# Window attention, then two expert layers: one weight conversion a chunk in the first block, its low part on VectorE, three conversions begun in the attention's last steps

## The chip, the cores and the metric

The kernel runs on one core of a Trainium2 chip. A core has a matrix engine (PE), a vector engine (DVE), an activation engine (ACT), a general engine (POOL) and an engine that only issues transfers (SP); each works through a queue of its own, in order, and waits on semaphores for the others. The metric is device time of one launch in microseconds (us), the median of three runs.

## The reference

Three stages follow one another, all in float32. The output of the first, transposed to 2304 tokens of 512 features, goes through two expert layers with a hidden width of 2048.

```python
scores = where(0 <= i - j < 128, q @ k.T / sqrt(64) + slope * -|i - j|, -1e9)   # 4 x 8 heads, 576 x 64
x = (softmax(scores) @ v).transpose(0, 2, 1, 3).reshape(2304, 512)

h = x @ moe_w_in                                        # first layer, 512 -> 2048
P = a[0] + a[1]*h + a[2]*h*h + a[3]*h*h*h
Q = 1 + |b[0]|*|h| + |b[1]|*h*h
x = (P / (Q + 1e-6)) @ moe_w_out                        # 2048 -> 512

h = x @ moe2_w_in                                       # second layer
out = where(h > 0, h, exp(min(h, 0)) - 1) @ moe2_w_out
```

The weights reach the kernel as float64 words: each weight is two 32-bit words, and the kernel makes a float32 value of them itself.

## The kernel before

**Split products.** Every large product is done in three passes of a reduced-precision float32 type: operands are split in a high part (a rounded copy) and a low part (operand minus high part), and high x high, low x high and high x low are summed in PSUM. So each operand of PE needs both parts before its group of matmuls can run.

**The weight tiles.** The first layer has 32 weight tiles, 16 of `w_in` ("wi", f = 0 to 15) and 16 of `w_out` ("wo"). A tile is loaded raw (512 KB) and converted by a chain: a scaled copy of the high words on ACT (`conv_scale`, line 174), a shift of the low words on DVE (`conv_shift`, line 182), shift-and-or of the two on DVE (`conv_or`, line 192), rounding to the high part on ACT (`conv_hi`, line 202), and the low part, a subtraction of two 128x512 operands (`conv_lo`, line 206), on POOL. The list `order` gives the sequence: wi0, wi1, wi2, wo0, wi3, wo1, wi4, and so on. Fifteen tiles are converted inside the attention stage, by steps of its hand-written queues. The other 17 are, in this order: wo6, wi9, wo7, wi10, wo8, wi11, wo9, wi12, wo10, wi13, wo11, wi14, wo12, wi15, wo13, wo14, wo15. They are left to `conv_step`. Each call of `conv_step` advances three tiles by a stage: it emits the rounding of the oldest and the scaled copy of a new one on ACT at once, and puts the low part of the oldest and the shift and or of the middle one in a list, `put_off`, out of which later code takes one at a time (`go_on`) or all. A tile whose scaled copy is in call n has its rounding and its low part in call n + 2, so 17 tiles take 19 calls.

**The first layer.** Tokens come in 5 blocks and the hidden width in 16 chunks of 128, so chunk s (0 to 79) is block s // 16, hidden rows s % 16. For each s the loop calls `gemm1(s)` (12 matmuls with tile wi, line 333), then `gemm2_T(s - 3)` (12 matmuls with tile wo, line 876), then `rational(s)`. PE runs them in this order: gemm1(s), gemm2_T(s - 3), gemm1(s + 1), and so on. The chunks 0 to 3 have their gemm1 in the attention's last steps already. `rational(s)` does, on ACT, four functions of h (lines 357 to 360) and, after DVE has the denominator (line 369), logarithm and exponential for the reciprocal (lines 372, 373); on DVE it finishes the previous chunk's quotient and its low part (lines 366, 377, 382; the last product, line 383, is on POOL from chunk 3 on) and the numerator of its own (lines 385, 386). In the first block it takes one put-off instruction at each of three places (ahead of line 366, ahead of line 377, and behind it). gemm2_T(s - 3) needs the high part of line 366 and the low part of line 383, both done in `rational(s - 2)`.

**Where the 17 conversions stand.** No call of `conv_step` at s = 0 and 1, two a chunk at s = 2 to 5, one a chunk at s = 6 to 16. At the last chunk of a block, `split_x` rounds the next block's x (ACT, line 312) and subtracts (two on DVE, two on POOL, line 313). From block 1 on, `joins` decides in which chunks weights of the second layer are prepared: none in chunks 0 and 15 of a block, none at s = 17 and s = 40. Their first three loads (`load_half`) are issued at s = 16. They use the three buffers that the conversions' scaled copies (`cvt`) used before.

**The order.** All engines' queues are written out by the program: in the attention by `QUEUES` (steps per engine, with a lag in units) and `NEEDS`, a loop that lets each step out once what it needs has been emitted; in the expert layers by the order of the calls. Steps of the attention that this text names: `r0c`, `r1a`, `XC` (ACT: parts of the first two rational functions, and a copy of attention output), `XY` (DVE: the copy of the last rows). A unit is one pair of heads, u = 0 to 15. `loads` issues the raw tiles: one a unit when a unit's q and k are done with (`load_some(1)`), four when u = 14 is done with v, the rest at u = 15.

Of the kernel before, what the change touches and what calls it, by code (L numbers as in the profile page):

```python
# [47 lines left out]
    "C10": (5,),  # L48
    "C11": (0, 3, 10, 11, 12, 14, 15),
}  # L50

ALL_S = ("S0", "S1", "S2", "S3", "S4")
NEEDS = {
# [34 lines left out]
def kernel(  # L88
# [14 lines left out]
    B, H, S, D = q.shape  # L103
# [8 lines left out]
    KF = DFF // P  # L112
# [30 lines left out]
    to_load, to_conv = order[:], order[:]  # L143
# [6 lines left out]
    def load_w(key):  # L150
        w, f = key
        w_in, w_out = ((w1_in, w1_out), (w2_in, w2_out))[f // KF]
        f %= KF
        RAW[key] = raw = place(key, [P, 2 * PC], I32, "raw")
        if w == "wi":
            nc.sync.dma_start(
                out=raw.rearrange("p (k c) -> p k c", k=KD),
                in_=w_in[:, f * P:(f + 1) * P].bitcast(I32).rearrange("(k p) c -> p k c", p=P),
            )
        else:  # L160
            nc.sync.dma_start(out=raw, in_=w_out[f * P:(f + 1) * P, :].bitcast(I32))
# [6 lines left out]
    def words(key):  # L168
        raw = RAW[key].rearrange("p (c t) -> p c t", t=2)
        return raw[:, :, 0], raw[:, :, 1]  # L170
# [5 lines left out]
    def conv_scale(key):  # L176
        T32[key] = t = cv_tile([P, PC], F32, "cvt")
        high = words(key)[1].bitcast(F32)
        scale_words(t, high)
# [6 lines left out]
    def conv_shift(key):  # L186
        shift(words(key)[0])

    def conv_or(key):
        low, _ = words(key)  # L190
        ti = T32[key].bitcast(I32)
        nc.vector.scalar_tensor_tensor(  # L192
            out=ti, in0=ti, scalar=3, in1=low, op0=ALU.logical_shift_left, op1=ALU.bitwise_or
        )

    def conv_hi(key, eng="A"):
        del RAW[key]
        WT[key] = w = place(key, [P, 2, PC], F32R, "w")
        if eng == "D":
            nc.vector.tensor_copy(w[:, 0], T32[key])  # L200
        else:
            nc.scalar.activation(out=w[:, 0], in_=T32[key], func=AF.Copy)

    def conv_lo(key, eng="G"):
        w, t = WT[key], T32.pop(key)
        (nc.vector if eng == "D" else nc.gpsimd).tensor_tensor(
            out=w[:, 1], in0=t, in1=w[:, 0].bitcast(F32), op=ALU.subtract
        )
# [4 lines left out]
    put_off = []  # L213

    def go_on():
        if put_off:
            put_off.pop(0)()

    def conv_step(keys, more=True, later=False, eng="A"):
        while put_off:  # L220
            go_on()
        if not (keys or stage["scaled"] or stage["whole"]):
            return
        new = keys.pop(0) if keys and more else None
        scaled, whole = stage["scaled"], stage["whole"]
        stage["scaled"], stage["whole"] = new, scaled
        if whole:
            conv_hi(whole, eng)
        if new:
            conv_scale(new)  # L230
        if whole:
            put_off.append(lambda: conv_lo(whole))
        if scaled:
            put_off.append(lambda: conv_shift(scaled))
            put_off.append(lambda: conv_or(scaled))
        while put_off and not later:
            go_on()

# [15 lines left out]
    WB = 512  # L254
# [27 lines left out]
    def width(c):  # L282
        return BL[c // KF][1]
# [39 lines left out]
    NCH = NB * KF  # L323
# [3 lines left out]
    def gemm1(c, f, x, b):  # L327

        conv_until(to_conv, ("wi", f))
        h_t[c] = h = bank(b, [P, width(c)], "h")  # L330
        for kk in range(KD):
            for n, (wp, xp) in enumerate(PASS):
                nc.tensor.matmul(  # L333
                    h, lhsT=WT["wi", f][:, SEL[wp], kk * P:(kk + 1) * P], rhs=x[xp][kk],
                    start=(kk == 0 and n == 0), stop=(kk == KD - 1 and n == 2),
                )
            yield

    def run_all(steps):
        for _ in steps:  # L340
            pass
# [88 lines left out]
    def attention():  # L430
        with ExitStack() as es:
# [6 lines left out]
            NU = len(units)  # L438
# [291 lines left out]
            def load_some(n):  # L730
                for _ in range(n):
                    load_w(to_load.pop(0))

            def loads(step, u):
                if step in ("qT", "kT", "zT") and {(n, u) for n in ("qT", "kT", "zT")} <= gone:
                    if u + 3 < NU:
                        load(u + 3, "qk")
                    if u < NU - 1:
                        load_some(1)
                    if u == 0:  # L740
                        nc.sync.dma_start(out=a_sb, in_=moe_a.partition_broadcast(P))
                        nc.sync.dma_start(out=b_raw, in_=moe_b.partition_broadcast(P))
                elif step in ("V0", "V1", "Y") and {(n, u) for n in ("V0", "V1", "Y")} <= gone:
                    if u + 2 < NU:
                        load(u + 2, "v")
                    else:
                        load_some(4 if u < NU - 1 else len(to_load))

            x1[0] = {}
            ahead = early()  # L750
# [41 lines left out]
            def warm(n):  # L792
                t = bank(3, [P, 4 * P], "warm")
                for _ in range(n):
                    nc.tensor.matmul(t, lhsT=zero[:, 0:P], rhs=zero, start=True, stop=True)
# [38 lines left out]
            def ready(step, u):  # L834
                wait = needs.get((step, u), []) + [
                    (n[0], u + n[1]) if isinstance(n, tuple) else (n, u) for n in NEEDS.get(step, ())
                ]
                return all(x in gone or not 0 <= x[1] < NU or not runs(*x) for x in wait)

            while any(queues.values()):  # L840
                for engine, queue in queues.items():
                    if queue and ready(*queue[0]):
                        step, u = queue.pop(0)
                        gone.add((step, u))
                        if step[0] in "xgro":
                            end_step(step)
                        elif step in CONV:
                            key = order[u - 1]
                            if step == "s0":
                                to_conv.remove(key)  # L850
                            CONV[step](key)
                        else:
                            RUN[step](u)
                        loads(step, u)
                        if (step, u) == ("kT", 0):
                            warm(1)
                        if (step, u) == ("E4", 2):
                            nc.scalar.activation(out=b_abs, in_=b_raw, func=AF.Abs)
# [7 lines left out]
    def experts():  # L866
# [29 lines left out]
        LAST = NCH - KF  # L896
# [15 lines left out]
        joined, half, two, whole, pair = {}, {}, {}, {}, []  # L912
# [32 lines left out]
        def join_shift(n):  # L945
            shift(half[n].rearrange("p (c t) -> p c t", t=2)[:, :, 0])
# [454 lines left out]
        def joins(s):  # L1401

            f = s % KF
            if s >= NCH or f in (0, KF - 1) or s in (KF + 1, 2 * KF + 8) or s < KF or width(s) < WB or s >= LAST + 3:
                return 0
            return 2 if s < LAST else 1

# [7 lines left out]
        for s in range(NCH):  # L1415
            o = s - SK
            j, f = divmod(s, KF)
            for _ in range(0 if s < 2 or s > KF else 2 if s < 6 else 1):
                conv_step(to_conv, later=True)
            if s >= 4:  # L1420
                run_all(gemm1(s, f, x1[j], (4, 5, 7)[(s - 4) % 3]))
            if f == KF - 1 and j + 1 < NB:
                x1[j + 1] = split_x(j + 1, lows="DDGG")
            if o >= 0:
                gemm2_T(o)
            if joins(s) == 2:

                def begin():
                    join_scale(nj + 1)
                    join_shift(nj)  # L1430

                rational(s, beside=(
                    begin, lambda: join_end(nj), lambda: join_shift(nj + 1), lambda: join_end(nj + 1),
                ))
            elif joins(s):
                rational(s, beside=(lambda: join_shift(nj), lambda: join_end(nj)) + 2 * (lambda: None,))
            elif s >= LAST:
                prepare(s)
            else:
                rational(s, beside=(go_on, lambda: None, go_on, go_on))  # L1440
            nj += joins(s)
            if s == KF:
                for n in range(3):
                    load_half(n)
            if joins(s + 1):
                join_scale(nj)
# [8 lines left out]
    with tc.manual_schedule():  # L1455
        attention()
        experts()
# [30 lines left out]
```

## Time and profile before

| | us |
|---|---|
| median of 3 runs (lowest, highest) | 935.35 (934.89, 935.69) |
| the profiled execution, whole | 935.59 |
| its span, first to last instruction | 933.8 |
| PE busy in the span | 912.6 (98%) |
| DVE busy | 785.1 (84%) |
| ACT busy | 706.3 (76%) |
| POOL busy | 225.0 (24%) |

All times in the text are microseconds from the start of the span of the one profiled execution. The attention takes the first 146 us, the first layer runs to about 545, the second layer to the end. A row of the timeline has the start, the length, the engine, the line, the operation with its operands, and, in brackets, how long the engine sat idle before it and who ended that. On DVE and ACT the next instruction starts a little before the one ahead has ended, so the text speaks of steps: from one start to the next.

### The profile page before, as it was taken

To read this page: it belongs to the slowest core of one execution; us is meant where nothing else is said; L and a number is where in the kernel's file an instruction comes from. 1 tells how busy PE (TensorE), PEld (TensorE's weight loads), DVE (VectorE), ACT (ScalarE), POOL (GpSimd) and SP (SyncE) were. 2 spreads that over 40 slices of the span, in tenths; PEclk is the share of its full clock that TensorE was granted. 3 is DMA by queue.
4 is the path that set the end of the run, shared out by engine and by line. 5 is a ranking of instruction groups with operands and counts; after the bars stand their busy time and mean duration, and the time that the engine had idled before them with its cause. 6 is when DMAs were issued, how large, how long until landed. Compare 5 with 4: busy or idle time off the path is not lost.

```text
span 933.8 us, 15528 instructions
## 1 busy us (share of the span) xinstructions
PE 912.6 (98%) x5110; PEld 774.7 (83%) x5110; DVE 785.1 (84%) x1709; ACT 706.3 (76%) x1500; POOL 225.0 (24%) x279
## 2 busy tenths in 40 slices
PE   8999998898999999999999999999999999999998
PEld 5777776686788888889988888898989888888887
DVE  7878887899899989997899889999968688777653
ACT  6898986888788888779887877675877567766553
POOL 4677782443422322232322210000000000000000
PEclk9999999899899999999999999999999999999999
DMA  9986647000155334410010133545243323442201
GB/s 194 205 201 167 161 139 271 1 1 0 52 152 159 113 92 146 131 62 1 1 35 0 38 93 99 167 158 194 88 158 105 121 80 102 147 147 79 80 1 67
DMA packets 112176, 98.27 MB, mean 105 GB/s; under 512 B 62432, under 2 KB 85984, under 8 KB 112096
## 3 DMA queue, kind: packets, MB, share of 16 engines
q1 hardware_dynamic: 109568, 96.56, 35.5%
q10 hardware_dynamic: 2528, 0.72, 0.4%
q8 instruction: 40, 0.66, 0.3%
q14 instruction: 40, 0.33, 0.1%
HBM read 79.96 MB, written 17.30 MB: 104 GB/s over the span
## 4 chain that ended last, share of the span: by engine, by line
PE 85%; DVE 11%; issue 2%; ACT 1%; POOL 1%; DVEq 0%; POOLq 0%; ACTq 0%
PE acc L1102 21%; PE m L1086 18%; PE acc L876 17%; PE h L333 17%; PE ps_pT L652 3%; PE s_ps L578 3%; PE x L671 3%; PE ps_qk L522 2%; DVE space_g L366 2%; DVE cvt L192 1%; DVE xT L369 1%; DVE xT L386 1%; DVE h L385 1%; DVE xT L382 1%; PE s_ps L560 1%
## 5 line engine op out<-in xcount | busy, mean ns | idle before, releaser
L876 PE MATMUL acc<-space_g,w_wo 128*128 128x512 f32 (+1 forms) x960 | 216.5, 374 | 8.6 <-POOL space_g L383 8.4
L876 PEld LDWEIGHTS acc<-space_g,w_wo 128*128 128x128 f32 x960 | 170.5, 192 | 42.4 <-POOL space_g L383 11.3
L383 POOL TENSOR_TENSOR space_g<-xT,space_r 128x512 fp32r<-128x512 f32 (+1 forms) x78 | 92.0, 1180 | 267.2 <-DVE xT L382 212.1
L1102 PE MATMUL acc<-op_wo,space_g 128*128 128x512 f32 x432 | 108.3, 393 | 0.0
L333 PE MATMUL h<-space_qa,w_wi 128*128 128x512 f32 (+1 forms) x320 | 93.0, 375 | 2.6 <-ACT space_qa L312 2.6
L1102 PEld LDWEIGHTS acc<-op_wo,space_g 128*128 128x128 f32 x432 | 80.5, 188 | 14.7
L1148 ACT ACTIVATE space_u<-space_r 128x384 f32<-128x384 f32 x48 | 25.1, 522 | 75.3 <-DVE space_r L1142 74.5
L1086 PE MATMUL m<-xo_wi,op_wi 128*128 128x384 f32 x336 | 77.3, 337 | 0.0
L333 PE MATMUL h<-space_qb,w_wi 128*128 128x512 f32 (+1 forms) x240 | 76.7, 374 | 0.5 <-DVE space_qb L313 0.5
L1086 PE MATMUL m<-xo_wo,op_wi 128*128 128x384 f32 x336 | 76.4, 335 | 0.0
L333 PE MATMUL h<-space_ta,w_wi 128*128 128x512 f32 (+1 forms) x240 | 76.2, 372 | 0.0
L357 ACT ACTIVATE space_u<-h 128x512 f32<-128x512 f32 (+1 forms) x78 | 43.0, 552 | 36.4 <-PE h L333 25.6
L369 DVE SCALAR_TENSOR_TENSOR xT<-space_u,b_abs,qa 128x512 f32<-128x512 f32 (+1 forms) x76 | 52.1, 685 | 21.7 <-ACT qa L358 21.6
L366 DVE TENSOR_TENSOR space_g<-xT,space_r 128x512 fp32r<-128x512 f32 (+1 forms) x79 | 65.1, 824 | 5.7
L333 PEld LDWEIGHTS h<-space_qa,w_wi 128*128 128x128 f32 x320 | 58.4, 191 | 13.1 <-ACT space_qa L312 3.0
L1086 PEld LDWEIGHTS m<-xo_wo,op_wi 128*128 128x128 f32 x336 | 60.9, 188 | 4.1
L372 ACT ACTIVATE space_r<-xT,c_q 128x512 f32<-128x512 f32 (+1 forms) x78 | 53.8, 690 | 11.6 <-DVE xT L369 11.5
L1086 PEld LDWEIGHTS m<-xo_wi,op_wi 128*128 128x128 f32 x336 | 60.6, 188 | 0.0
L333 PE MATMUL h<-space_bi,w_wi 128*128 128x512 f32 (+1 forms) x160 | 59.6, 372 | 1.0 <-DVE space_bi L764 0.8
L1152 ACT ACTIVATE space_u<-space_u,c_m 128x384 f32<-128x384 f32 x96 | 57.5, 611 | 1.6
L359 ACT ACTIVATE xT<-h,a_sb 128x512 f32<-128x512 f32 (+1 forms) x78 | 57.6, 738 | 0.0
L360 ACT ACTIVATE h<-h,a_sb 128x512 f32<-128x512 f32 (+1 forms) x78 | 55.9, 716 | 0.0
(209 smaller groups left out, 2132.4 us busy)
## 6 DMA issues: line engine op xcount, KB each, us to landing
space_qa<-joined_wo SPq DMA_DIRECT2D x43, 256.0 KB, 2.7
raw_wo<-in_moe_w_out_dram SPq DMA_DIRECT2D x20, 512.0 KB, 5.2
raw_wi<-in_moe_w_in_dram SPq DMA_DIRECT2D x16, 512.0 KB, 4.9
half<-in_moe_w_in_dram SPq DMA_DIRECT2D x32, 256.0 KB, 2.7
two_wo<-joined_wi SPq DMA_DIRECT2D x32, 256.0 KB, 2.9
s<-sums SPq DMA_DIRECT2D x32, 256.0 KB, 2.7
half<-in_moe_w_out_dram SPq DMA_DIRECT2D x22, 256.0 KB, 2.9
v<-in_v_dram SPq DMA_DIRECT2D x32, 128.0 KB, 3.3
```

Of the source, the lines that this page charges most:

```text
L333: nc.tensor.matmul(h, lhsT=WT["wi", f][:, SEL[wp], kk * P:(kk + 1) * P], rhs=x[xp][kk], start=(kk == 0 and n == 0), stop=(kk == KD - 1 and ...
L357: nc.scalar.activation(out=h2, in_=h, func=AF.Square)
L359: nc.scalar.activation(out=ee, in_=h, func=AF.Identity, scale=a_sb[:, 1:2], bias=a_sb[:, 0:1])
L360: nc.scalar.activation(out=h, in_=h, func=AF.Identity, scale=a_sb[:, 3:4], bias=a_sb[:, 2:3])
L366: nc.vector.tensor_tensor(out=hi, in0=ee0, in1=rr0, op=ALU.mult)
L369: nc.vector.scalar_tensor_tensor(out=qq, in0=h2, scalar=b_abs[:, 1:2], in1=qa, op0=ALU.mult, op1=ALU.add)
L372: nc.scalar.activation(out=rr, in_=qq, func=AF.Ln, bias=c_q)
L383: (nc.gpsimd if c > 2 else nc.vector).tensor_tensor(out=low, in0=ee0, in1=rr0, op=ALU.mult)
L876: nc.tensor.matmul(acc_t[d], lhsT=WT["wo", f][:, SEL[wp], d * P:(d + 1) * P], rhs=gt[SEL[xp]], start=(f == 0 and n == 0), stop=(f == KF - ...
L1086: nc.tensor.matmul(out, lhsT=w[:, SEL[wp], c0:c0 + P], rhs=XO[q // NP2, nm, k][:, SEL[xp]], start=(k == 0 and n == 0), stop=(k == 1 and n ...
L1102: nc.tensor.matmul(acc_t[T, t], lhsT=gt[SEL[xp]][:, t * P:(t + 1) * P], rhs=w[:, SEL[wp]], start=(first and n == 0), stop=(last and n == 2),)
L1152: nc.scalar.activation(out=e, in_=e, func=AF.Identity, bias=c_m)
```

## The change

The low part of the 17 tiles that `conv_step` handles goes from POOL to DVE and stands behind the shift and the or in the put-off list. Three calls of `conv_step` are made in the attention, behind the steps `r0c`, `r1a` and `XC` of unit 15, and what they put off is emitted behind `XY` of unit 15. In the first layer there is one call a chunk at s = 2 to 17, in place of two a chunk at s = 2 to 5 and one at 6 to 16. Raw tiles 12 to 17 of the list are loaded a little earlier: two a unit at u = 11 to 13, two rather than four at u = 14. `load_half` begins at s = 17, the chunks 17 and 18 are without joins, and chunk 40 now has two.

```diff
+CONV_AFTER = (("r0c", 15), ("r1a", 15), ("XC", 15))
...
         if new:
             conv_scale(new)
-        if whole:
-            put_off.append(lambda: conv_lo(whole))
         if scaled:
             put_off.append(lambda: conv_shift(scaled))
             put_off.append(lambda: conv_or(scaled))
+        if whole:
+            put_off.append(lambda: conv_lo(whole, "D"))
...
-                        load_some(1)
+                        load_some(2 if 10 < u < 14 else 1)
...
-                        load_some(4 if u < NU - 1 else len(to_load))
+                        load_some(2 if u < NU - 1 else len(to_load))
...
+                        if (step, u) in CONV_AFTER:
+                            conv_step(to_conv, later=True)
+                        if (step, u) == ("XY", NU - 1):
+                            while put_off:
+                                go_on()
...
-            if s >= NCH or f in (0, KF - 1) or s in (KF + 1, 2 * KF + 8) or s < KF or width(s) < WB or s >= LAST + 3:
+            if s >= NCH or f in (0, KF - 1) or s in (KF + 1, KF + 2) or s < KF or width(s) < WB or s >= LAST + 3:
...
-            for _ in range(0 if s < 2 or s > KF else 2 if s < 6 else 1):
+            if 2 <= s <= KF + 1:
                 conv_step(to_conv, later=True)
...
-            if s == KF:
+            if s == KF + 1:
                 for n in range(3):
                     load_half(n)
```

PE's instructions stand in the same order in both programs. What moves is on DVE, ACT, POOL and SP. The added lines shift line numbers by 2 in the changed program up to the queues' loop and by 7 behind it: line 366 is 368 there, line 206 is 208.

DVE behind the attention, before: line 427 is chunk 0's last product, and the next rows are the first of chunk 2 (chunk 1's own part is done in the attention).

```order
L411 TENSOR_TENSOR h<-space_u,h 128x512
L412 TENSOR_TENSOR xT<-xT,h 128x512
L427 TENSOR_TENSOR space_g<-xT,space_r_75 128x512
L182 TENSOR_SCALAR raw_wo_2121<-raw_wo_2121 128x512
L366 TENSOR_TENSOR space_g<-xT,space_r_76 128x512
L369 SCALAR_TENSOR_TENSOR xT<-space_u,b_abs,xT 128x512
```

The same place in the changed program: `raw_wi_1692` and `cvt_2183` are tile wi9, `cvt_2139` is wo6, and `raw_wo_1811` is wo7.

```order
L413 TENSOR_TENSOR h<-space_u,h 128x512
L414 TENSOR_TENSOR xT<-xT,h 128x512
L429 TENSOR_TENSOR space_g<-xT,space_r_75 128x512
L184 TENSOR_SCALAR raw_wi_1692<-raw_wi_1692 128x512
L194 SCALAR_TENSOR_TENSOR cvt_2183<-cvt_2183,raw_wi_1692 128x512
L208 TENSOR_TENSOR w_wo_2258<-cvt_2139,w_wo_2258 128x512
L184 TENSOR_SCALAR raw_wo_1811<-raw_wo_1811 128x512
L368 TENSOR_TENSOR space_g<-xT,space_r_76 128x512
L371 SCALAR_TENSOR_TENSOR xT<-space_u,b_abs,xT 128x512
```

Shift and or of wi9 and the low part of wo6 have come in between chunk 0's last product and the shift of chunk 2. Shift and or of wo6 stand further ahead, right behind the step XY. On ACT the rounding of wi9 now stands ahead of chunk 2's functions of h.

DVE in one chunk of the middle of the block, before:

```order
L366 TENSOR_TENSOR space_g<-xT,space_r_75 128x512
L369 SCALAR_TENSOR_TENSOR xT<-space_u,b_abs,qa 128x512
L182 TENSOR_SCALAR raw_wo_2233<-raw_wo_2233 128x512
L377 SCALAR_TENSOR_TENSOR xT<-xT,space_g 128x512
L192 SCALAR_TENSOR_TENSOR cvt_2451<-cvt_2451,raw_wo_2233 128x512
L382 TENSOR_TENSOR xT<-xT 128x512
L385 TENSOR_TENSOR h<-space_u,h 128x512
L386 TENSOR_TENSOR xT<-xT,h 128x512
```

DVE in chunk 14 and at the begin of chunk 15 in the changed program: `w_wi_2810` is tile wi15, the operand of gemm1(15); the two rows of line 315 are the split of the next block's x.

```order
L184 TENSOR_SCALAR raw_wo_2251<-raw_wo_2251 128x512
L368 TENSOR_TENSOR space_g<-xT,space_r_76 128x512
L371 SCALAR_TENSOR_TENSOR xT<-space_u,b_abs,qa 128x512
L194 SCALAR_TENSOR_TENSOR cvt_2766<-cvt_2766,raw_wo_2251 128x512
L379 SCALAR_TENSOR_TENSOR xT<-xT,space_g 128x512
L208 TENSOR_TENSOR w_wi_2810<-cvt_2720,w_wi_2810 128x512
L384 TENSOR_TENSOR xT<-xT 128x512
L387 TENSOR_TENSOR h<-space_u,h 128x512
L388 TENSOR_TENSOR xT<-xT,h 128x512
L315 TENSOR_TENSOR space_qb<-xT,space_qa 128x512
L315 TENSOR_TENSOR space_ta<-xT,space_qa 128x512
L184 TENSOR_SCALAR raw_wo_2253<-raw_wo_2253 128x512
```

A chunk has nine DVE instructions rather than eight; the shift stands ahead of line 368, and the low part (line 208) between lines 379 and 384.

POOL near the end of the block before, where `w_wi_2771` is tile wi15, and line 383 is in turn the one of chunks 12, 13 and 14:

```order
L383 TENSOR_TENSOR space_g<-xT,space_r_76 128x512
L206 TENSOR_TENSOR w_wi_2771<-cvt_2681,w_wi_2771 128x512
L383 TENSOR_TENSOR space_g<-xT,space_r_75 128x512
L206 TENSOR_TENSOR w_wo_2817<-cvt_2727,w_wo_2817 128x512
L383 TENSOR_TENSOR space_g<-xT,space_r_76 128x512
```

In the changed program POOL has only the rows of line 385 (383 before) there and the two of the split; the low part of wi15 has gone from ahead of chunk 13's row to the middle of chunk 14 on DVE.

## Rows read from the trace of the kernel before

**Rows 1.** Waits of PE, 145 to 245 us: total, times, longest.
```profile
PE acc L876 <- POOL space_g L383: 8.4, 6, 3.2
PE h L333 <- ACT space_qa L312: 2.6, 1, 2.6
```

**Rows 2.** Windows: length, then PE, PEld, DVE, ACT, POOL busy, granted clock, DMA.
```profile
160.00:180.00 20.00, 14.45 (x52) 11.18 (x53) 15.82 (x23) 14.53 (x25) 10.39 (x8) 0.86 0.01 2
180.00:190.00 10.00, 10.00 (x36) 8.02 (x35) 9.80 (x16) 8.03 (x14) 3.38 (x3) 0.77 0.00 0
...
230.00:240.00 10.00, 7.45 (x18) 5.01 (x19) 9.97 (x14) 7.64 (x14) 6.09 (x4) 0.66 0.08 25
```

**Rows 3.** Timeline of PE, first block and start of the second.
```profile
152.00 2.88 PE L876 MATMUL acc<-space_g,w_wo 128*128 128x512 f32 x12
...
186.40 2.88 PE L876 MATMUL acc<-space_g,w_wo 128*128 128x512 f32 x12
...
191.84 2.88 PE L876 MATMUL acc<-space_g,w_wo 128*128 128x512 f32 x12
...
223.19 0.61 PE L333 MATMUL h<-space_qa,w_wi 128*128 128x512 f32 x2
...
244.21 2.88 PE L876 MATMUL acc<-space_g,w_wo 128*128 128x512 f32 x12
```

**Rows 4.** Timeline of DVE, one chunk (s = 9) and the start of the next.
```profile
196.50 1.80 DVE L366 TENSOR_TENSOR space_g<-xT,space_r 128x512 fp32r<-128x512 f32 x1
198.23 0.73 DVE L369 SCALAR_TENSOR_TENSOR xT<-space_u,b_abs,qa 128x512 f32<-128x512 f32 x1
198.89 0.42 DVE L182 TENSOR_SCALAR raw_wo<-raw_wo 128x512 int32<-128x512 int32 x1
199.22 0.68 DVE L377 SCALAR_TENSOR_TENSOR xT<-xT,space_g 128x512 f32<-128x512 f32 x1
199.83 0.68 DVE L192 SCALAR_TENSOR_TENSOR cvt<-cvt,raw_wo 128x512 int32<-128x512 int32 x1
200.43 0.68 DVE L382 TENSOR_TENSOR xT<-xT 128x512 f32<-128x512 f32 x1
201.03 0.68 DVE L385 TENSOR_TENSOR h<-space_u,h 128x512 f32<-128x512 f32 x1
201.75 0.69 DVE L386 TENSOR_TENSOR xT<-xT,h 128x512 f32<-128x512 f32 x1
202.57 1.80 DVE L366 TENSOR_TENSOR space_g<-xT,space_r 128x512 fp32r<-128x512 f32 x1
```

**Rows 5.** Timeline of POOL: chunk 3's end, chunk 9, tile wi15.
```profile
159.90 1.27 POOL L383 TENSOR_TENSOR space_g<-xT,space_r 128x512 fp32r<-128x512 f32 x1 [3.39 <-DVE xT L382]
...
196.47 1.29 POOL L206 TENSOR_TENSOR w_wi<-cvt,w_wi 128x512 fp32r<-128x512 f32 x1
201.28 1.30 POOL L383 TENSOR_TENSOR space_g<-xT,space_r 128x512 fp32r<-128x512 f32 x1 [3.52 <-DVE xT L382]
...
220.68 1.31 POOL L206 TENSOR_TENSOR w_wi<-cvt,w_wi 128x512 fp32r<-128x512 f32 x1
```

**Rows 6.** Timeline of DVE in block 1, without a conversion's low part on POOL.
```profile
268.38 0.68 DVE L366 TENSOR_TENSOR space_g<-xT,space_r 128x512 fp32r<-128x512 f32 x1
```

**Rows 7.** Timeline of DVE, chunk 0's last product, chunk 3, chunk 4's shift.
```profile
146.12 0.68 DVE L427 TENSOR_TENSOR space_g<-xT,space_r 128x512 fp32r<-128x512 f32 x1
...
156.78 0.75 DVE L369 SCALAR_TENSOR_TENSOR xT<-space_u,b_abs,xT 128x512 f32<-128x512 f32 x1 [1.71 <-ACT xT L358]
...
160.92 0.53 DVE L182 TENSOR_SCALAR raw_wi<-raw_wi 128x512 int32<-128x512 int32 x1
```

**Rows 8.** Timeline of ACT, a conversion's rounding at chunk 3.
```profile
154.50 0.63 ACT L202 ACTIVATE w_wi<-cvt 128x512 fp32r<-128x512 f32 x1 [2.24 <-DVE cvt L192]
```

**Rows 9.** Timeline of DVE, the split of x at chunk 15.
```profile
232.64 0.75 DVE L313 TENSOR_TENSOR space_qb<-xT,space_qa 128x512 fp32r<-128x512 f32 x1
...
236.68 0.73 DVE L369 SCALAR_TENSOR_TENSOR xT<-space_u,b_abs,qa 128x512 f32<-128x512 f32 x1
```

## The prediction

> **What bounds the kernel now.** I read PE's busy share first (98% of the span: little to win in general), then PE's waits. From 145 to 245 us, the first block of the first layer, PE waits 8.4 us in six places for POOL's line 383, and 2.6 for the rounded x of the next block [rows 1]. The windows show what these waits also cost: the granted clock is 0.86, 0.77 and 0.66 there [rows 2], so PE ran partly at 1.2 instead of 2.4 GHz. Taken as 0.14 x 20 + 0.23 x 10 + 0.34 x 10 = 8.5 us for the three waits of 2.6 to 3.2, a long wait is followed by up to some 2.8 us lost.
>
> Then the timelines. A pair of groups (gemm1 and gemm2_T, 24 matmuls) takes PE 191.84 - 186.40 = 5.44 [rows 3], 2.72 a group. A chunk on DVE takes 202.57 - 196.50 = 6.07 [rows 4]. So DVE is the slow one of the two; PE, which runs ahead of it by the three chunks of delay, in the end waits for what DVE and POOL hand over. PE's 24 matmuls from 152.00 (gemm2_T(1)) to 244.21 (gemm2_T(14)) are 13 pairs, 70.7 us of work in 92.2 [rows 3]. At most 21.5 us are to be had here. From 244.21 on I take both programs as equal.
>
> In the DVE chunk one row stands out: line 366 takes 1.80 [rows 4], and 0.68 in block 1 [rows 6]. It begins at 196.50, POOL's line 206 (the low part of a weight tile) at 196.47, for 1.29 [rows 5]; line 366 goes on only when that ends.
>
> **The change, part by part.**
>
> *Low part from POOL to DVE.* A 128x512 instruction on two SBUF operands has a step of 0.60 on DVE (199.83 to 200.43, [rows 4]); the low part adds one a chunk. Line 366 without POOL beside it has the 0.68 of [rows 6], so a step of 0.60 instead of 1.73. What is left on POOL is line 383, from 0.85 behind the start of line 382 (200.43, 201.28) for 1.3 [rows 4, 5]. It runs beside lines 385 and 386, which did not lengthen, and overlaps the shift, which now comes next. At 160.92 such a shift took 0.53 instead of 0.42, beside line 383 of 159.90 [rows 4, 5, 7]: 0.11 more. Chunk in steps: shift 0.33 + 0.11, line 366 0.60, line 369 0.66, or 0.60, line 377 0.60, low part 0.60, line 382 0.60, line 385 0.72, line 386 0.60: 5.42. Bounds: 5.31 without any overlap; 6.55 if line 366 keeps its 1.73. I take 5.42, the nearest rows.
>
> The Trainium skill (SBUF — State Buffer, Who interferes with whom) says that of a VectorE and a GpSimd instruction that need the shared port pair the one that starts later fully blocks, `tensor_scalar` in its two-port modes included. By that the shift would wait 0.2 for the end of line 383, a chunk would be 5.5 and the whole 1 us longer; the 0.11 measured at 160.92 decides.
>
> *The start.* Line 427 starts at 146.12 [rows 7]. Behind it: shift of wi9 at 146.73 (0.42, and 0.04 until the or, which waits for it), or at 147.2 to 147.9, then the low part of wo6. ACT's rounding of wi9 waits for that or, and chunk 2's functions of h are queued behind it, so it isn't hidden. From the rounding to line 369 it is 156.78 - 154.50 = 2.28 in chunk 3 before [rows 7, 8], so line 369 of chunk 2 is at 150.2. Chunk 2 (its line 383 is on DVE): 0.66 + 0.60 + 0.60 + 0.60 + 0.72 + 0.60 + 0.72 + 0.60 + 0.33 + 0.60 = 6.0, so line 369 of chunk 3 is at 156.2; before it was 156.78 [rows 7]. The single conversion wins nothing up to there, the two more in chunks 3 to 5 do later. Shift and or of wo6, some 1.1 us, fall in a gap of DVE in which it waits for PE; without that cover they would cost 1.1. The three scaled copies on ACT likewise.
>
> *Eleven chunks* follow: line 369 of chunk 14 at 156.2 + 11 x 5.42 = 215.8.
>
> *The wait that is late next.* gemm1(15) needs the low part of wi15. Before, POOL did it at 220.68, done 1.2 us ahead of gemm1(15) at 223.19 [rows 3, 5]. Now its call comes one chunk later, and it stands in the middle of chunk 14 on DVE: 215.8 + 0.66 + 0.60 + 0.60 + 0.68 = 218.4. PE would be there far earlier: it gets the low part of chunk 1 at 154.1, of chunk 2 at 160.9 (line 382 at 158.7, + 0.85 + 1.3), so gemm2_T(3) starts at 165.9, and from there DVE keeps PE's pace; gemm1(15) would stand at 165.9 + 8 x 5.44 + 2.72 = 212.1. So PE waits some 6 us, the first 0.9 already in gemm1(14) for wi14. Queued behind it is all of PE; nothing on DVE waits for it before chunk 15. The wait is the difference of PE's lead and DVE's place and costs PE's lead alone, so DVE's chain up to 218.4 sets the time.
>
> *To the end of the block.* From 218.4: 11 matmuls of gemm1(15), 2.5, then gemm2_T(12), gemm1(16), gemm2_T(13), gemm1(17), 4 x 2.72 = 10.9; gemm2_T(14) at 231.8. The split of x: from the first subtraction to line 369 it is 236.68 - 232.64 = 4.04 [rows 9], now with a shift in between, 0.33; it begins at 220.2 (lines 382, 385, 386 of chunk 14 behind the low part), so line 369 of chunk 15 is at 224.6 and the low part of wo13 at 227.1, 0.6 behind gemm2_T(13) at 226.5. And a wait of 6 us brings the half clock: I take the 2.8 from above, which hides the 0.6. gemm2_T(14) at 231.8 + 2.8 = 234.6; before 244.21 [rows 3]. That is 9.6 us less; 11.8 with the full clock (the 0.6 then counts).
>
> *Loads, joins.* The tiles that are needed earlier are also loaded one or more units (7 us) earlier; the first half loads are one chunk later, and so is their first use. Chunk 40 has the DVE work that its neighbours have beside PE. I take nothing for these, between -1 and +1.
>
> Sum: 935.59 - 9.6 = 926.0 for the profiled execution, which was 0.24 above the median, so 925.8.
>
> **The rivals.**
>
> *The clock holds, or PE's lead is not used up.* If a chunk on DVE were 5.31 or less, and the wait at gemm1(15) short, the clock would stay at 2.4 GHz and the split would not be late: 11 x 0.11 = 1.2 and 2.2 for the clock more, and 1 to 2 of the start: 921. For it: chunks in block 1 run without a gap. Against: wi15 stands a chunk later in any case.
>
> *Line 383 delays more than the shift.* If line 366 also loses some 0.2 each chunk, 5.62: 11 x 0.2 = 2.2, and two or three longer waits of PE at half clock; 929 to 930. For it: the shift's neighbour now is just line 366. Against: line 383 ends 2.15 behind the start of line 382, line 366 comes at 2.36.
>
> *The load on DVE decides: slower.* If line 366's 1.80 is not POOL's line 206 but line 366's own place behind line 386, the chunk is 6.55. Then line 369 of chunk 14 is at 228.3, wi15's low part at 230.9, gemm2_T(14) at 230.9 + 13.4 + 2.8 = 247.1, 2.9 later: 938.5. It decides from a chunk of 6.29 on (2.9 / 11 less). For it: DVE is busy for 9.80 and 9.97 of 10 us in two windows of the block [rows 2], and 17 instructions go onto it. Against: [rows 6].
>
> The Trainium skill (Perfetto Trace Analysis, Optimizing Scalar/DVE Operations) says that work of a saturated DVE may well be taken off it, even to GPSIMD, which speaks for this rival; and that between those two it might not help since they share a port, which speaks against it. Rows 5 and 6 agree with the second half.
>
> *It doesn't do what it says.* PE's part of the wait is only moved: what DVE gains up to chunk 14 comes back at wi15, wo13 and the split with a half clock through both groups, and the sum is within 0.2% (1.9 us, about what a measurement of this kernel can tell from no change): 934 to 937. Against: the six waits were DVE's pace, and that is faster by 0.65 a chunk.
>
> **How the numbers follow.** Forecast (922.5 to 928.5): 0.62. Clock or lead better: 0.12. Line 383 delays more: 0.13. Nothing gained: 0.06. Slower: 0.07. Faster by over 0.2%: 0.62 + 0.12 + 0.13 = 0.87; within: 0.06; slower: 0.07. The range leaves out the last two and the far end of the first rival: 920 to 931.5.
>
> **What would show it.** Right: line 366's row at 0.68 in the first block, DVE chunks of 5.4, line 369 of chunk 3 near 156; one long wait of PE in gemm1(15), for line 208 of DVE, of 5 to 6.5, with a granted clock of half behind it; waits for POOL's line 385 down to one or two near 154 and 160; gemm2_T(14) near 234.6. Wrong: line 366 still at 1.8, a wait for raw tiles or for ACT's rounding, or no wait at wi15.

## The result

The changed kernel takes 926.31 us (median of 4 runs, 926.18 to 926.45) and the one before, beside it, 935.52 (934.89 to 936.55): ratio 0.9900, interval 0.9883 to 0.9918. The forecast was 925.8 in 920 to 931.5, faster; it held. The profiled execution took 926.45 (span 924.7, mean granted clock 0.996) against 935.59 (933.8, 0.991): 9.14 us less.

PE's waits of the first block, 145 to 245 us, after (total, times, longest); before there were six for POOL and one for ACT [rows 1], and two of 0.5 and 0.2 for DVE:

```profile
PE h L335 <- DVE w_wi L208: 5.0, 2, 4.7
PE acc L883 <- DVE space_g L385: 1.7, 1, 1.7
PE acc L883 <- POOL space_g L385: 1.2, 1, 1.2
```

One long wait is left, and it names DVE's line 208, the low part that the change has put there. The windows after (length, PE, PEld, DVE, ACT, POOL busy, granted clock, DMA share, GB/s), to be held against [rows 2]:

```profile
160.00:180.00 20.00, 18.86 (x83) 15.56 (x84) 19.86 (x34) 17.99 (x30) 4.97 (x4) 1.00 0.01 1
180.00:190.00 10.00, 10.00 (x46) 8.29 (x45) 9.93 (x18) 8.88 (x16) 2.60 (x2) 1.00 0.00 0
...
210.00:220.00 10.00, 5.21 (x19) 3.79 (x18) 9.93 (x18) 9.29 (x16) 1.93 (x2) 0.90 0.00 1
220.00:230.00 10.00, 10.00 (x35) 7.95 (x34) 7.77 (x14) 6.37 (x12) 4.62 (x4) 0.76 0.00 0
230.00:240.00 10.00, 10.00 (x45) 8.26 (x44) 9.40 (x15) 7.82 (x13) 2.40 (x2) 1.00 0.29 81
```

Three stretches of half clock have become one, behind the one wait. In PE's timeline after (start, length, in brackets the idle time before), beside [rows 3]:

```profile
154.22 2.56 PE L883 MATMUL acc<-space_g,w_wo 128*128 128x512 f32 x10 [1.69 <-DVE space_g L385]
...
166.25 2.88 PE L883 MATMUL acc<-space_g,w_wo 128*128 128x512 f32 x12
...
218.63 0.80 PE L335 MATMUL h<-space_qa,w_wi 128*128 128x512 f32 x1 [4.69 <-DVE w_wi L208]
...
229.58 2.88 PE L883 MATMUL acc<-space_g,w_wo 128*128 128x512 f32 x12
...
235.02 2.88 PE L883 MATMUL acc<-space_g,w_wo 128*128 128x512 f32 x12
```

gemm2_T(14) starts at 235.02 instead of 244.21 [rows 3]: 9.19 us, which is the whole difference of the two executions (9.14). From there on they run alike: to the end it is 689.59 us before and 689.68 after, with PE busy for 685.2 in both.

A DVE chunk after (s = 10) with the shift of the next, beside [rows 4]:

```profile
199.21 0.68 DVE L368 TENSOR_TENSOR space_g<-xT,space_r 128x512 fp32r<-128x512 f32 x1
199.81 0.73 DVE L371 SCALAR_TENSOR_TENSOR xT<-space_u,b_abs,qa 128x512 f32<-128x512 f32 x1
200.47 0.68 DVE L194 SCALAR_TENSOR_TENSOR cvt<-cvt,raw_wi 128x512 int32<-128x512 int32 x1
201.07 0.68 DVE L379 SCALAR_TENSOR_TENSOR xT<-xT,space_g 128x512 f32<-128x512 f32 x1
201.68 0.68 DVE L208 TENSOR_TENSOR w_wo<-cvt,w_wo 128x512 fp32r<-128x512 f32 x1
202.28 0.68 DVE L384 TENSOR_TENSOR xT<-xT 128x512 f32<-128x512 f32 x1
202.88 0.68 DVE L387 TENSOR_TENSOR h<-space_u,h 128x512 f32<-128x512 f32 x1
203.59 0.69 DVE L388 TENSOR_TENSOR xT<-xT,h 128x512 f32<-128x512 f32 x1
204.20 0.51 DVE L184 TENSOR_SCALAR raw_wo<-raw_wo 128x512 int32<-128x512 int32 x1
204.62 0.68 DVE L368 TENSOR_TENSOR space_g<-xT,space_r 128x512 fp32r<-128x512 f32 x1
```

Line 368 (366 before) takes 0.68 instead of 1.80, and a chunk 204.62 - 199.21 = 5.41 instead of 6.07, though it has one instruction more.

### The profile page after: what moved, and what is told of

It reads as the page before. It is cut to its first block, busy times and chain, and to the rows that moved or that the text cites. A ratio compares the mean times of both kernels' runs of the same rounds, so it can differ in the third digit from the quotient of the medians.

```text
span 924.7 us, 15509 instructions
## 1 busy us (share of the span) xinstructions
PE 906.8 (98%) x5110; PEld 771.9 (83%) x5110; DVE 780.1 (84%) x1726; ACT 705.3 (76%) x1500; POOL 202.9 (22%) x262
## 4 chain that ended last, share of the span: by engine, by line
PE 91%; DVE 6%; POOL 1%; issue 1%; ACT 1%; POOLq 0%; DVEq 0%; ACTq 0%
PE acc L1109 21%; PE acc L883 20%; PE h L335 20%; PE m L1093 19%; PE ps_pT L654 3%; PE s_ps L580 3%; PE x L673 3%; PE ps_qk L524 2%; PE s_ps L562 1%; PE ty L684 1%; DVE pr_wo L606 0%; DVE cvt L194 0%; PE ty L538 0%; DVE xT L379 0%; POOL space_bi L315 0%
## 5 line engine op out<-in xcount | busy, mean ns | idle before, releaser
L883 PE MATMUL acc<-space_g,w_wo 128*128 128x512 f32 (+1 forms) x960 | 211.9, 369 | 3.0 <-DVE space_g L385 1.7
L883 PEld LDWEIGHTS acc<-space_g,w_wo 128*128 128x128 f32 x960 | 168.6, 189 | 34.4 <-DVE space_g L385 2.1
L385 POOL TENSOR_TENSOR space_g<-xT,space_r 128x512 fp32r<-128x512 f32 (+1 forms) x78 | 92.2, 1182 | 294.2 <-DVE xT L384 212.1
L368 DVE TENSOR_TENSOR space_g<-xT,space_r 128x512 fp32r<-128x512 f32 (+1 forms) x79 | 52.6, 666 | 4.6 <-ACT qa L360 0.5
```

The lines of the kernel that those rows point to most:

```text
L368: nc.vector.tensor_tensor(out=hi, in0=ee0, in1=rr0, op=ALU.mult)
L385: (nc.gpsimd if c > 2 else nc.vector).tensor_tensor(out=low, in0=ee0, in1=rr0, op=ALU.mult)
L883: nc.tensor.matmul(acc_t[d], lhsT=WT["wo", f][:, SEL[wp], d * P:(d + 1) * P], rhs=gt[SEL[xp]], start=(f == 0 and n == 0), stop=(f == KF - ...
```

## The experiments

My theory: DVE's pace in the block, and the moment at which its last low parts are done, set the time; the low part on DVE sets the pace, the earlier start of the conversions sets the moment; what is left is PE's wait for wi15 and the half clock behind it. Rivals: one half of the change does it alone; the loads and joins have a share. Ratios are against runs of the kernel before on the same chip (medians 935.5 to 935.7).

**The low part alone.** Kernel before, with the low part on DVE behind the or; still two conversions in chunks 2 to 5, none begun in the attention.

```diff
-        if whole:
-            put_off.append(lambda: conv_lo(whole))
         if scaled:
             put_off.append(lambda: conv_shift(scaled))
             put_off.append(lambda: conv_or(scaled))
+        if whole:
+            put_off.append(lambda: conv_lo(whole, "D"))
```

> The kernel before, with one part of the change: the low parts of the 17 tiles go to VectorE, behind the or; two conversions a chunk in chunks 2 to 5 stay. My theory (VectorE's line 366 was held up by POOL's line 206, and VectorE's pace sets the block): line 366 at 0.68 us in the whole first block, a VectorE chunk of 5.4 instead of 6.07 from chunk 6 on, so 8 x 0.65 = 5.2 us earlier at chunk 14, PE's small waits from 214 us on gone and the half clock at the change of block with them; gemm2_T(14) at 235 to 236 instead of 244.2, about 927 us in all. Rival (the gain comes from spreading the conversions, and the seventeen instructions only load VectorE): 935 to 940 us.

928.19 us, ratio 0.9920 (0.9906 to 0.9934): 7.3 us less, so the rival is out. It is 1.2 more than expected: at the change of block PE still waits 2.5 us in three places for the split, with a clock of 0.91 and 0.92 in 220:240, and the expectation had these waits as gone. DVE chunks with one conversion are 5.41 to 5.42 long, with two 8.0 to 8.3: line 369, and then the two longest waits of PE.

```profile
148.59 0.75 DVE L369 SCALAR_TENSOR_TENSOR xT<-space_u,b_abs,xT 128x512 f32<-128x512 f32 x1 [0.84 <-ACT xT L358]
...
156.88 0.75 DVE L369 SCALAR_TENSOR_TENSOR xT<-space_u,b_abs,xT 128x512 f32<-128x512 f32 x1 [0.88 <-ACT xT L358]
...
165.02 0.75 DVE L369 SCALAR_TENSOR_TENSOR xT<-space_u,b_abs,qa 128x512 f32<-128x512 f32 x1 [0.85 <-ACT qa L358]
```
```profile
161.67 2.60 PE L876 MATMUL acc<-space_g,w_wo 128*128 128x512 f32 x10 [3.62 <-POOL space_g L383]
...
169.67 4.14 PE L876 MATMUL acc<-space_g,w_wo 128*128 128x512 f32 x10 [2.22 <-POOL space_g L383]
```

PE waits 6.5 us in three places for line 383 (8.4 before); the name is POOL's, the lateness DVE's, whose chunk hands POOL its operand. gemm2_T(14) is at 237.14.

**The schedule alone.** The changed kernel with the low part back on POOL. It stays behind the or in the put-off list, as in the run above, so what that place does by itself is in both halves.

```diff
             put_off.append(lambda: conv_or(scaled))
         if whole:
-            put_off.append(lambda: conv_lo(whole, "D"))
+            put_off.append(lambda: conv_lo(whole))
```

> The changed kernel with the low parts of the 17 tiles back on POOL, so only the schedule is changed. My theory: line 368 stays at 1.8 us, a chunk at 6.05, chunk 14's line 371 at 156.3 + 11 x 6.05 = 222.9, the low part of wi15 late for gemm1(15) by some 4 us with a half clock behind; gemm2_T(14) near 238, about 929.5 us. With e1 that is more than the whole change gives, since both take the same slack of PE. Rival (the two parts add up): e1 and e2 together gain 9.2 us. Second rival (the schedule is all of it): 926.3 us.

930.40 us, ratio 0.9944 (0.9931 to 0.9957): 5.1 us less, 0.9 short of what was expected. DVE and POOL side by side at one chunk's begin, and PE at gemm1(15):

```profile
197.31 1.78 DVE L368 TENSOR_TENSOR space_g<-xT,space_r 128x512 fp32r<-128x512 f32 x1
```
```profile
197.06 1.48 POOL L208 TENSOR_TENSOR w_wi<-cvt,w_wi 128x512 fp32r<-128x512 f32 x1
```
```profile
219.84 0.50 PE L335 MATMUL h<-space_qa,w_wi 128*128 128x512 f32 x1 [2.00 <-ACT w_wi L204]
222.68 0.79 PE L335 MATMUL h<-space_qa,w_wi 128*128 128x512 f32 x1 [2.33 <-POOL w_wi L208]
```

Line 368 is as long as before and DVE's chunk 6.01 to 6.04. 7.3 and 5.1 make 12.4, the two together 9.2: they aren't additive. Either one takes time out of the same waits, and with both the first chunks are no longer what is late, but wi15.

**Loads and joins alone.** Kernel before with these four lines of the change.

```diff
-                        load_some(1)
+                        load_some(2 if 10 < u < 14 else 1)
...
-                        load_some(4 if u < NU - 1 else len(to_load))
+                        load_some(2 if u < NU - 1 else len(to_load))
...
-            if s >= NCH or f in (0, KF - 1) or s in (KF + 1, 2 * KF + 8) or s < KF or width(s) < WB or s >= LAST + 3:
+            if s >= NCH or f in (0, KF - 1) or s in (KF + 1, KF + 2) or s < KF or width(s) < WB or s >= LAST + 3:
...
-            if s == KF:
+            if s == KF + 1:
```

> The kernel before with only the edits that the prediction took at nothing: earlier loads of raw tiles 12 to 17, load_half one chunk later, chunks 17 and 18 without joins and chunk 40 with two. My theory: 935.5, within 1 us. Rival (earlier loads delay v and q, or chunk 40 gets too full): 936.5 to 939.

935.71 us, ratio 1.0002 (0.9993 to 1.0011): nothing.

**The half clock taken away.** The changed kernel with 22 more matmuls of 128x512 into gemm1(15)'s own bank ahead of it (which is started anew behind them).

```diff
+        if c == KF - 1:
+            for _ in range(22):
+                nc.tensor.matmul(h, lhsT=WT["wi", f - 1][:, 0, 0:P], rhs=x["hi"][0], start=True, stop=True)
```

> The changed kernel with 22 matmuls of 128x512 more, on operands that are there, into the bank that gemm1(15) is about to write (it starts anew, so they leave nothing behind): 22 x 0.227 = 5.0 us of work inside the wait of gemm1(15). My theory (the wait ends with the low part of wi15 and costs another 3.0 us by the half clock behind it): the granted clock stays at 2.4 GHz, the low part lands at the same 218.6, gemm2_T(14) at 232.0 to 232.8 instead of 235.0, 923.5 to 924 us. Rival (the half clock costs nothing since VectorE's chain, with the low part of wo13, is late anyway): 926 us. Slower if the extra matmuls end behind the low part: 926.5 to 927.5.

924.31 us, ratio 0.9881 (0.9867 to 0.9895): 2.0 us less than the changed kernel. The window at full clock, and gemm2_T(13), which had no wait of its own before:

```profile
220.00:230.00 10.00, 9.62 (x43) 7.65 (x42) 9.96 (x14) 7.31 (x13) 5.11 (x4) 1.00 0.01 2
```
```profile
227.48 2.79 PE L886 MATMUL acc<-space_g,w_wo 128*128 128x512 f32 x11 [0.38 <-DVE w_wo L208]
...
232.82 2.88 PE L886 MATMUL acc<-space_g,w_wo 128*128 128x512 f32 x12
```

gemm2_T(14) comes 2.20 earlier. The half clock took 3.0 us of the changed kernel (218.63 to 229.58 is 10.95, against 2.5 + 2.72 x 2 = 7.94 at full clock); without it wo13 is late, as the forecast had it, and gives part back.

**Each wi ahead of its wo.** The changed kernel with seven neighbours of `to_conv` swapped.

```diff
     to_load, to_conv = order[:], order[:]
+    for n in range(15, 28, 2):
+        to_conv[n], to_conv[n + 1] = to_conv[n + 1], to_conv[n]
```

> The changed kernel with seven pairs of tiles swapped in the order of conversion: each of wi9 to wi15 is converted before the wo tile that stood ahead of it, so that wi15's low part is made in chunk 13 instead of 14 and wo12's a chunk later. My theory (the 4.69 us wait of the second layer's half h for wi15's low part, and the half clock behind it, are what the change still leaves): the wait in gemm1(15) falls to about 0.5 us, the clock stays near 1 in 210:230, gemm2_T(12) now waits some 2.8 us for wo12 and gemm2_T(13) for wo13 until about 227.4; gemm2_T(14) begins at about 232.5 against 235.02, and the run takes 924 us (923 to 926). Rival: the wait is only handed from wi15 to wo12, with the same half clock behind it: gemm2_T(14) at about 235 and 926 us.

924.30 us, ratio 0.9883 (0.9867 to 0.9900); gemm2_T(14) at 232.79. The waits came as forecast, 2.39 for wo12 and 1.43 for wo13; the clock was 0.96 and 0.87 in 210:230, so the wait was not handed on at its full price.

**A fourth tile begun in the attention.** The changed kernel with one call more there and one less behind.

```diff
-CONV_AFTER = (("r0c", 15), ("r1a", 15), ("XC", 15))
+CONV_AFTER = (("r0a", 15), ("r0c", 15), ("r1a", 15), ("XC", 15))
...
-            if 2 <= s <= KF + 1:
+            if 2 <= s <= KF:
```

> The changed kernel with a fourth tile begun in the attention's last steps, and so fourteen chunks with a conversion instead of fifteen: every low part is made one chunk earlier. My theory (the end of the first block is set by the day on which the conversions finish): the wait for wi15's low part is gone, no half clock in 210:230, gemm2_T(14) at about 230.5 against 235.02, and the run takes about 922 us, if the fourth shift, or and low part fit into VectorE's idle time ahead of the first chunk's chain (late by 0 to 0.6 us). Rival: VectorE has no room there, its chain begins 1.6 us or more later, every chunk with it, and the gain shrinks to 0 to 2 us: 924 to 926 us.

924.40 us, ratio 0.9880 (0.9865 to 0.9894): a miss by 2.4, inside the range of the rival. Of the wait for wi15 only 0.3 us is left in gemm1(15), but DVE's chain (line 424) begins at 143.27 instead of 141.99, and PE now waits 2.5 us for the split, with a clock of 0.83 behind it.

**Both.** The fourth tile and the swapped neighbours in one kernel, by the two edits above.

> The fourth tile and the swapped pairs together. If both waits (wi15 and the wo tiles behind it) are gone with the fourth tile alone, the swap adds nothing: within 0.5 us of the kernel with the fourth tile. If the fourth tile leaves a wait for wi15, the swap takes 1 to 2 us more off; if a swapped wo tile is now the late one, it costs up to 1 us.

924.37 us, ratio 0.9881 (0.9866 to 0.9896): the swap adds nothing to the fourth tile. Four different cures stop at 924.3 to 924.4, so something else is late there. In each of the four, at the block's end, a DVE row of 0.68 takes 1.76 to 1.78 and the shift 1.49 to 1.52. DVE and POOL in the kernel with the swapped pairs:

```profile
221.10 1.76 DVE L317 TENSOR_TENSOR space_ta<-xT,space_qa 128x512 fp32r<-128x512 f32 x1
222.78 1.52 DVE L186 TENSOR_SCALAR raw_wo<-raw_wo 128x512 int32<-128x512 int32 x1
```
```profile
220.96 1.35 POOL L317 TENSOR_TENSOR space_bi<-xT,space_qb 128x512 fp32r<-128x512 f32 x1 [0.33 <-ACT space_qb L316]
222.27 1.75 POOL L317 TENSOR_TENSOR space_bi<-xT,space_ta 128x512 fp32r<-128x512 f32 x1
```

POOL's two subtractions of the split stretch a subtraction on DVE from 0.69 to 1.76 and the shift from 0.42 to 1.52: the same collision that the change has taken out of line 366. So I put them on DVE as well, for the second block's split only:

```diff
-                x1[j + 1] = split_x(j + 1, lows="DDGG")
+                x1[j + 1] = split_x(j + 1, lows="DDDD" if j == 0 else "DDGG")
```

With the swapped pairs:

> The kernel with the swapped pairs, and all four low parts of the second block's split on VectorE instead of two on GpSimd. That kernel came out at 924.3 us, as did the ones with the fill and with the fourth tile; in all three VectorE's work at the block's end runs beside GpSimd's two subtractions and is stretched: a split's subtraction 1.76 us instead of 0.69, the shift behind it 1.52 instead of 0.42. My theory (this is the new bound, since chunk 15's line 373 and the low part of wo13 stand behind it): two subtractions more cost VectorE 1.2 us and 2.1 us of stretch go; line 373 of chunk 15 starts at about 223.9 against 224.82, gemm2_T(13) gets wo13 at 226.5 instead of 227.42, gemm2_T(14) starts at about 231.9 against 232.79, and the run takes 923.4 us. Rival: VectorE's time at the block's end isn't the bound, or the subtractions cost more than the stretch: 924.3 to 925.5.

923.34 us, ratio 0.9875 (0.9858 to 0.9891); line 373 of chunk 15 at 223.85, gemm2_T(13) goes on at 226.45, gemm2_T(14) starts at 231.79, 0.05, 0.05 and 0.11 earlier than expected. With the fourth tile:

> The kernel with the fourth tile, and all four low parts of the second block's split on VectorE. There TensorE waits 2.5 us in the second block's first half h for parts of the split, and gets half a clock behind it. My theory: the parts come at 222.4, 223.0, 223.6 and 224.2 (the second was at 224.16, the last at 225.3), gemm2_T(13) starts at 226.3 to 226.6 against 227.37, gemm2_T(14) at about 232 against 232.90, and the run takes 923.4 us; a little less if the clock stays up. Rival: TensorE waits for the split until VectorE's chunk has ended anyway and the half clock stays: 924.3 to 925.

922.62 us, ratio 0.9862 (0.9847 to 0.9877). This median lies between two pairs: 921.83 and 921.91, with a mean granted clock of 1.000, and 923.33 and 923.47, with 0.998. The profiled execution is the one of 923.47 (923.4 expected), with gemm2_T(13) at 226.18, gemm2_T(14) at 232.00 and a clock of 0.83 in 220:230.

**The same with a fill ahead of the second block's first h.** 8 matmuls on a weight tile where PE waits for the split.

```diff
+        if c == KF:
+            for _ in range(8):
+                nc.tensor.matmul(h, lhsT=WT["wi", f][:, 0, 0:P], rhs=WT["wi", f][:, 0, 0:width(c)], start=True, stop=True)
```

> The kernel with the fourth tile and all four low parts on VectorE, with 8 extra 128x512 matmuls on a weight tile into the second block's first bank ahead of its h, where TensorE waits 1.8 us for the split's parts; the bank is started anew behind them, so they add nothing to a result. There gemm1(16) took 5.5 us (220.65 to 226.18) instead of 2.72, at half a clock. My theory: the clock stays at 1.00 in 220:230, gemm1(16) goes as the parts come (the last at 224.3), gemm2_T(13) starts at about 224.9 instead of 226.18, gemm2_T(14) at 230.4 to 230.8 instead of 232.00, and the run takes 921.2 to 921.6 instead of 922.6 us. Rival: VectorE's chain holds gemm2_T(13) and (14) anyway, and the time stays within 0.4 of 922.6.

921.85 us (921.76 to 921.93), ratio 0.9851 (0.9837 to 0.9864): the best version of this study, 4.5 us below the changed kernel. Clock 1.00 in 220:230, and gemm2_T(13), (14):

```profile
224.90 2.88 PE L886 MATMUL acc<-space_g,w_wo 128*128 128x512 f32 x12
...
230.34 2.88 PE L886 MATMUL acc<-space_g,w_wo 128*128 128x512 f32 x12
```

gemm2_T(14) has moved by 1.66, and the profiled execution is 923.47 - 921.85 = 1.62 shorter. The medians differ by 0.8 only, because two of the four executions without the fill took 921.8 to 921.9 already. So the fill does not beat the better executions; with it all five are like them.

**The shift back behind line 371.** The changed kernel with another order of the put-off steps.

```diff
-                rational(s, beside=(go_on, lambda: None, go_on, go_on))
+                rational(s, beside=(lambda: None, lambda: None, go_on, lambda: (go_on(), go_on())))
```

> The changed kernel with the shift of a chunk back behind line 371, so that line 368, a product of two operands in SBUF, is what follows line 388 and meets the end of GpSimd's line 385. In the changed kernel the shift there took 0.51 us instead of 0.42 and ended 0.29 behind GpSimd; line 368 beside GpSimd's low part (the kernel with it back on GpSimd) ended 0.54 behind it. Theory A (VectorE's instruction gets through its first 0.13 us and then stands until GpSimd has ended, whichever instruction it is): line 368 takes about 0.77 instead of 0.68, a VectorE chunk stays at 5.41, and the time at 926.3. Theory B (only the shift loses something): 5.32 a chunk, the low part of wi15 1.0 us earlier (216.9), 925.3. Theory C (line 368 loses the whole overlap of 0.22 or more): 5.5 a chunk or more, wi15's low part 1 to 2 us later, 927 to 928.

927.44 us, ratio 0.9910 (0.9897 to 0.9924): 1.1 us more than the changed kernel, a chunk of 5.55, wi15's low part at 219.85. These are theory C's numbers, but not its cause:

```profile
155.14 0.69 DVE L388 TENSOR_TENSOR xT<-xT,h 128x512 f32<-128x512 f32 x1
155.93 0.69 DVE L368 TENSOR_TENSOR space_g<-xT,space_r 128x512 fp32r<-128x512 f32 x1
...
199.56 0.69 DVE L388 TENSOR_TENSOR xT<-xT,h 128x512 f32<-128x512 f32 x1
200.38 0.69 DVE L368 TENSOR_TENSOR space_g<-xT,space_r 128x512 fp32r<-128x512 f32 x1
```

Line 368 is not stretched. It starts 0.82 behind line 388, whose result it reads; at 155.14, in a chunk whose line 385 is on DVE and POOL is idle, it is 0.79. An independent instruction in between has a step of 0.61 (203.59 to 204.20 above). So the shift's new place fills a gap of some 0.2 a chunk, which [rows 4] show before as well (201.75 to 202.57). That gap kept line 368 out of the collision, so line 368 doesn't tell the three theories apart. Another row of this run does, the first subtraction of the split, which also reads two operands in SBUF:

```profile
221.30 1.28 POOL L385 TENSOR_TENSOR space_g<-xT,space_r 128x512 fp32r<-128x512 f32 x1 [4.29 <-ACT cvt L176]
```
```profile
222.38 0.76 DVE L315 TENSOR_TENSOR space_qb<-xT,space_qa 128x512 fp32r<-128x512 f32 x1
```

It overlaps line 385 by 0.20 and takes 0.76 instead of 0.68, ending 0.56 behind it. That is theory A; theory B would leave it at 0.68, theory C would make it 0.88.

## Why the prediction was right, point by point

*Line 366 and the chunk.* 0.68 forecast and measured, step 0.60; chunk 5.42 against 5.41. The 0.60 that it took for line 386 rests on the shift behind it, which it did not say: with line 368 there it is 0.82.

*The shift beside POOL.* 0.11 forecast; measured 0.42 - 0.33 = 0.09, so size and sum were right. The reason was half wrong: the forecast took the 0.11 as evidence against blocking. The Trainium skill (SBUF — State Buffer, Who interferes with whom) says that of two instructions that need the shared pair the later one fully blocks. The ends of the rows agree with that: POOL's line 385 ran from 203.12 (below) to 204.42, the shift ended at 204.71, 0.29 later; [rows 5, 7] give 161.17 and 161.45, 0.28; the split above 224.02 and 224.30, 0.28, although POOL ran on for 1.24 there. Likewise line 368: 0.54 behind POOL's end in [rows 4, 5], 0.55 in the schedule alone. So of 0.42 and of 0.68 some 0.13 is as good as done before the block, and the loss is the overlap less 0.13. Where POOL's row lies after:

```profile
203.12 1.30 POOL L385 TENSOR_TENSOR space_g<-xT,space_r 128x512 fp32r<-128x512 f32 x1 [4.12 <-DVE xT L384]
```

*The start, the chain, the late wait.* Chunk 2's line 369 (371 after) at 150.2, chunk 3's at 156.2, wi15's low part done at 218.4: measured 150.28, 156.35 and 217.89 + 0.68 = 218.57.

```profile
150.28 0.75 DVE L371 SCALAR_TENSOR_TENSOR xT<-space_u,b_abs,xT 128x512 f32<-128x512 f32 x1 [0.88 <-ACT xT L360]
...
156.35 0.74 DVE L371 SCALAR_TENSOR_TENSOR xT<-space_u,b_abs,xT 128x512 f32<-128x512 f32 x1
...
217.89 0.68 DVE L208 TENSOR_TENSOR w_wi<-cvt,w_wi 128x512 fp32r<-128x512 f32 x1
...
225.00 0.75 DVE L371 SCALAR_TENSOR_TENSOR xT<-space_u,b_abs,qa 128x512 f32<-128x512 f32 x1 [1.97 <-ACT qa L360]
```

PE was to wait some 6 us in two places; it was 5.0. gemm2_T(3) came nearly on time (165.9, 166.25), but gemm1(15) began at 213.44 instead of 212.1. gemm2_T(3) gave 0.35 of that; the wait for wi14's low part in gemm1(14) put gemm2_T(11) back by 0.6 (the forecast had this wait, at 0.9, but left it out of its 212.1); and the first matmul of gemm1(15) waited 0.3 for the high part of wi15, which ACT had ready at 213.38, a wait that the forecast didn't have. It cost nothing, as PE's lead is lost in the wait anyway.

*The half clock.* 2.8 taken from the waits of before; 3.0 measured, and the fill shows that the net price was 2.0 to 2.2, as wo13 was late behind it. That the half clock hid wo13's 0.6 was right.

*The split.* Line 369 (371) of chunk 15 was forecast at 224.6 and came at 225.00, but that it came so near is luck. The 4.04 taken from [rows 9] holds two rows that POOL's subtractions stretch to 1.76; first they are shown before, then after, where POOL's subtractions come later:

```profile
233.32 1.76 DVE L313 TENSOR_TENSOR space_ta<-xT,space_qa 128x512 fp32r<-128x512 f32 x1
235.00 1.76 DVE L366 TENSOR_TENSOR space_g<-xT,space_r 128x512 fp32r<-128x512 f32 x1
```
```profile
221.40 0.69 DVE L315 TENSOR_TENSOR space_ta<-xT,space_qa 128x512 fp32r<-128x512 f32 x1 [0.22 <-ACT space_qa L314]
...
222.34 0.68 DVE L368 TENSOR_TENSOR space_g<-xT,space_r 128x512 fp32r<-128x512 f32 x1
```

The 2.15 us saved there went into a step that the forecast didn't have: DVE waited 0.22 and 1.97 us for ACT. ACT writes the next block's x over the parts that gemm1(15) still reads, and gemm1(15) was at half clock. The last three of four roundings each wait 0.65 for it:

```profile
220.74 0.63 ACT L314 ACTIVATE space_qa<-xT 128x512 fp32r<-128x512 f32 x1 [0.65 <-PE h L335]
```

*gemm2_T(14)* at 234.6: 235.02. *Loads and joins* at nothing: 0.02% alone.

*The rivals.* The slower one (DVE's own load decides) falls with the low part alone: 17 instructions more on DVE, and 7.3 us less. Its condition, that line 366's 1.80 comes from its place behind line 386, falls with two runs: in the schedule alone the shift stands between and line 368 takes 1.78, and with the shift moved back line 368 follows line 388 at once and takes 0.69. "Nothing gained" falls with the 9.2 us. Of the two that lie to either side, line 368 beside line 385 did not come true; the better clock is what the fills made, 924.31 alone and 921.85 with the fourth tile and the split on DVE, against that rival's 921.

## What to carry to other kernels

Where an instruction takes far longer in one place than in another, look at what a neighbouring engine runs at that time before you count its load: a busy engine can become faster by taking the disturber's work over. Gains of two halves that draw on the same waits do not add; measure each alone and name what is late when both are in. When several cures stop at the same time, look for what their traces have in common.

## What was not expected

A blocked VectorE instruction ends a fixed time behind GpSimd's (0.28 to 0.29 for a shift of 0.42, 0.54 to 0.56 for a product or a subtraction of 0.68), so an overlap of 0.2 costs only 0.08 to 0.09. Lines 387 and 388, with one operand in PSUM, ran beside the same GpSimd instruction at 0.68 to 0.69.

The half clock behind a wait of about 5 us does not have one price: 3.0 us behind 4.69 in the changed kernel; with the shift moved back gemm1(15) waited 4.99 until 220.59, and gemm2_T(13) began at 230.37, 9.78 later instead of 10.95: 1.8 us. So versions may differ by 1.2 us through that price alone.
